# No dummy products at the attention's end, and one store for a tile's two left blocks

## The chip, the cores and the metric

The kernel runs on one core of one Trainium2 chip. The metric is the device time of one execution, in microseconds. TensorE (PE) multiplies matrices into PSUM, VectorE (DVE) and ScalarE (ACT) work on PSUM and SBUF, GpSimd (POOL) takes part in the attention, and SyncE (SP) and ScalarE issue DMAs from their queues.

## The reference

An attention with a feature map is followed by two MLPs, all in float32. It has 4 batches, 8 heads, 576 positions and 64 columns for each head; the MLPs see 2304 tokens of 512 features and have 2048 hidden features.

```python
def phi(x):
    proj = np.einsum('bhsd,df->bhsf', x, w_phi)
    proj = proj - np.max(np.abs(proj), axis=-1, keepdims=True)
    return np.concatenate([np.exp(proj), np.exp(-proj)], axis=-1)
q_p, k_p = (phi(q), phi(k))
kv = np.einsum('bhsf,bhsd->bhfd', k_p, v)
z = np.sum(k_p, axis=2)
num = np.einsum('bhsf,bhfd->bhsd', q_p, kv)
den = np.einsum('bhsf,bhf->bhs', q_p, z)[..., None] + 1e-06
x = num / den                                # then to (tokens, 512)
h = x @ w_in;  x = np.maximum(0.01 * h, h) @ w_out
h = x @ w2_in; y = (h * np.tanh(softplus(h))) @ w2_out
```

## The kernel before

**The attention** goes through 16 pairs of heads, `attention(n)` for n = 0 to 16, software-pipelined: a call does the projections of one pair, the sums of the next older and the output of the one before. A batch's first 512 positions are its main part; the last 64 are its left tokens. Products are made three times, from a high and a low part of each operand (`three`, L94 to L97), so that float32 is kept. `split`, `high` and `low` make the parts: a copy on ScalarE (L273) and a subtraction on VectorE (L277).

**The MLPs' products** are done by a seven-product scheme (Strassen-Winograd) over halves of features and tokens. An item n is one pair of 128-feature blocks f with one pair of batches sb. It uses four PSUM banks: X (product `p1`, A11 x B11), Z (`p7`, S3 x T3), Y and W. `seed_y` (ScalarE) copies X into Y; `keep_p7` (ScalarE) copies Z to SBUF (z7); `join_w` (VectorE) makes W = Y + z7. Then products are added on: S2 x T2 to Y and A12 x B21 to X (after which `head2` reads X out), A22 x T4 to W (`tail4`), S1 x T1 to Y (`tail5`, read out as Y + z7 by VectorE), S4 x B22 to Y (`tail3`). A read-out goes through the activation (`leaky`, L906) on ScalarE and is stored to DRAM by ScalarE's queue a step later. `c_item(f)` does the left tokens of all four batches, split into ch and cl, for the two blocks of f; it takes a bank of its own. The first items are (f, sb) = (0, 0), (1, 0), then c_item(0), c_item(1), then (0, 1), (1, 1).

**PSUM** has eight banks. During the attention, ring "a" has four, and the attention's own tiles the other four (pool `pa`); when the attention is done, these become ring "b" (pool `pb`). X, Z and the left tokens take ring "a", Y and W ring "b". A bank that is asked for when all of a ring are taken is one whose last reader must end first. The program order is the code's order on each engine; work that is not of the products (weight conversions, splits, sums, stores) is put between them in steps, by chains with costs and gates and by `later(n, f)`, which runs f n steps on.

**Around the attention's end.** In the last pairs' calls, `fill(0)` does p1 and p7 of item 0 and `fill(1)` its S2 x T2 and A12 x B21; `extra` (at == 1, n == PAIRS - 1) emits seed_y(0) and keep_p7(0). Behind the loop come p1(1), the last transposes `x_t(15)`, p7(1), and the release of the attention's pools. `touch(t)` is a dummy product of 512 columns into a bank, whose result is overwritten: one in fill(0) on item 0's Y, and four, L962 to L964, on the first four banks of ring "b". Then come seed_y(1), keep_p7(1), join_w(0), head2(0), and in `first` cycle(1): tail4(0), tail5(0), S2 x T2 and A12 x B21 of item 1, tail3(0), and c_item(0).

**The end.** The last products are those of the left tokens of the second MLP. A tile `left_out[t]` holds 128 rows: the 64 left tokens of batch 2t and those of batch 2t + 1. Its parts are added by VectorE (L1660), and `left_store(t)` stores it (L1666): rows 0 to 63 from SyncE's queue, rows 64 to 127 from ScalarE's. In DRAM the two blocks are 576 rows apart.

Of the kernel before, what the change touches and what calls it, by code (L numbers as in the profile page):

```python
# [9 lines left out]
F32 = mybir.dt.float32  # L10
F32R = mybir.dt.float32r
AF = mybir.ActivationFunctionType
ALU = mybir.AluOpType
# [7 lines left out]
def attention_two_mlps_kernel(  # L21
# [12 lines left out]
    nc = tc.nc  # L34
    B, H, S, D = q.shape
# [3 lines left out]
    P = 128  # L39
    KD = DM // P  # L40
    M = DFF // P
    MAIN = 512
    NM = MAIN // P
    LEFT = S - MAIN
# [26 lines left out]
    dr = tc.alloc_tile_pool(name="dr", bufs=1, space=bass.MemoryType.DRAM)  # L71
# [15 lines left out]
    def bank(ring):  # L87
        return rings[ring].tile([P, 512], F32, tag=ring, name=ring)
# [16 lines left out]
    class Places:  # L105
# [23 lines left out]
        def drop(self, t):  # L129
# [5 lines left out]
    places = Places([Places.Word(lambda i=i: two_words[:, i]) for i in range(2)] + [Places.Word(lambda: place("c", F32, DM, pool=gp))],  # L135
                    [Places.Word(lambda i=i: place("st%d" % i, I32, DM, 2, pool=gp, name="stage")) for i in range(2)])
# [111 lines left out]
    A11, A12, A22, S3, S1, S2, S4 = range(OPS)  # L248
# [32 lines left out]
    B11, T3, T2, B21, T1, T4, B22 = range(OPS)  # L281
    win = {}
# [27 lines left out]
    with tc.manual_schedule():  # L310
# [244 lines left out]
        def x_t(i):  # L555
            s = st[i]
            b, p = divmod(i, NP)
            t = pa.tile([P, 512], F32, tag="xt", name="xt")
            xn = s["xn"].rearrange("p c m d -> p (c m d)")
            for j in range(NM):  # L560
                nc.tensor.transpose(out=t[:, j * P:(j + 1) * P], identity=ident,  # L561
                                    in_=xn[:, j // 2 * 6 * D + j % 2 * P:][:, 0:P])
            o = st[min(i + 1, PAIRS - 1)]["kvp"][:, MAIN - LEFT:MAIN]
            nc.tensor.matmul(out=o, lhsT=xn[:, 4 * D:4 * D + P], rhs=eyes, start=True, stop=True)
            nc.scalar.activation(out=XC[:, p, b * LEFT:(b + 1) * LEFT], in_=o, func=AF.Copy)
            if i < PAIRS - 1:
                st[i] = None
            return lambda: nc.scalar.activation(out=xmain(p, b), in_=t, func=AF.Copy)
# [159 lines left out]
        def extra(n, at):  # L728
            for when, d in ((0, top), (1, mid), (2, end)):
                if at == when and n in d:  # L730
                    d[n]()
            for i, step in STEPS.get((n, at), ()):
                conv[i][step]()
            if at == 1 and n == PAIRS - 1:
                seed_y(0)
                keep_p7(0)

# [75 lines left out]
        def later(n, f):  # L815
            due.append((pos[0] + n, f))
# [9 lines left out]
        one = Layer()  # L826
# [4 lines left out]
        def weights(f, w):  # L831
            i, x = {A11: (0, 0), A12: (0, 1), A22: (1, 0), S3: (2, 0), S1: (2, 1), S2: (3, 0), S4: (3, 1)}[w]
            need(cur[0].mark[0], f, i)
            return [t[:, x * E:(x + 1) * E].rearrange("p (q n) -> p q n", q=2) for t in cur[0].wt[f, i]]
# [11 lines left out]
                three(t, h[:, i], l[:, i], xh[:, i], xl[:, i], start=(start and i == 0), stop=(i == 1),  # L846
                      skip_group_check=True)

        def touch(t):

            nc.tensor.matmul(out=t, lhsT=weights(0, A11)[0][:, 0], rhs=win[0, B11][0][:, 0],
                             start=True, stop=True)

        def p1(n):
            cur[0].it[n]["X"] = bank("a")
            prod(n, cur[0].it[n]["X"], A11, B11, True)

        def p7(n):
            cur[0].it[n]["Z"] = bank("a")
            prod(n, cur[0].it[n]["Z"], S3, T3, True)  # L860

        def seed_y(n):
            nc.scalar.activation(out=cur[0].it[n]["Y"], in_=cur[0].it[n]["X"], func=AF.Copy)

        def keep_p7(n):
            nc.scalar.activation(out=cur[0].z7[n % 2], in_=cur[0].it[n].pop("Z"), func=AF.Copy)

        def fill(part):
            if part == 0:
                p1(0)  # L870
                p7(0)
                it[0]["Y"] = bank("a")
                touch(it[0]["Y"])
            else:
                prod(0, it[0]["Y"], S2, T2, False)
                prod(0, it[0]["X"], A12, B21, False)
# [4 lines left out]
            attention(n)  # L881
        loads.held = False
        p1(1)
        x_t(PAIRS - 1)()
        p7(1)
        ap.release()
        pa.release()
        rings["b"] = tc.alloc_tile_pool(name="pb", bufs=4, space=PSUM)
# [31 lines left out]
        def join_w(n):  # L920
            x = cur[0].it[n]
            charge()
            nc.vector.tensor_tensor(out=x["W"], in0=x["Y"], in1=cur[0].z7[n % 2], op=ALU.add)
# [6 lines left out]
        def head2(n):  # L930
            cur[0].out((2 * cur[0].it[n]["f"], 2 * cur[0].it[n]["sb"]), cur[0].it[n]["X"])
# [13 lines left out]
        def c_half(f, t, i):  # L945
            need(cur[0].mark[1], "c", 0)
            need(cur[0].mark[1], "c", 1)
            b1, b2 = ([x[:, s] for x in cur[0].cw] for s in (slice(0, 2), slice(2, 4)))
            todo = [(w, o, q_) for w, o in (((A11, b1), (A12, b2)), ((S1, b1), (A22, cur[0].dw)))[i] for q_ in range(2)]
            for x, (w, o, q_) in enumerate(todo):  # L950
                h, l = weights(f, w)
                three(t[:, i * NC:(i + 1) * NC], h[:, q_], l[:, q_], o[0][:, q_], o[1][:, q_],
                      start=(x == 0), stop=(x == 3))

        def c_item(f, *between, g=None):
            t = bank("a")
# [2 lines left out]
                do()  # L959
            cur[0].out((f, B), t, g)  # L960

        it[0]["W"], it[1]["Y"], it[1]["W"], it[2]["Y"] = (bank("b") for _ in range(4))  # L962
        for t in (it[0]["W"], it[1]["Y"], it[1]["W"], it[2]["Y"]):
            touch(t)  # L964
        seed_y(1)
        keep_p7(1)
        join_w(0)
        head2(0)
        low(one.cw + [XC])
        nc.vector.tensor_tensor(out=XC[:, 0:2], in0=XC[:, 2:4], in1=XC[:, 0:2], op=ALU.subtract)  # L970

# [192 lines left out]
        def cycle(n):  # L1164
            it_ = cur[0].it
            x, begun = it_[n], "X" in it_[n]
            if n:
                tail4(n - 1)
                used(n - 1, 0, 1)
                work()  # L1170
            if not begun:
                p1(n)
            if "Y" not in x:
                x["Y"] = bank("b")
            if not begun:
                seed_y(n)
            work()
            if not begun:
                p7(n)
                keep_p7(n)  # L1180
            work()
            if n:
                tail5(n - 1)
                used(n - 1, 2)
                work()
            prod(n, x["Y"], S2, T2, False)
            if "W" not in x:
                x["W"] = bank("b")
            join_w(n)
            work()  # L1190
            prod(n, x["X"], A12, B21, False)
            head2(n)
            work()
            if n:
                tail3(n - 1)
                used(n - 1, 3)
                work()
# [462 lines left out]
            nc.vector.tensor_tensor(out=natural(left_out[t], h), in0=a, in1=b, op=ALU.add)  # L1660

        def left_store(t):
            o = left_out[t]
            for r in range(2):
                b = 2 * t + r
                (nc.sync, nc.scalar)[r].dma_start(out=out[b * S + MAIN:(b + 1) * S, :], in_=o[r * LEFT:(r + 1) * LEFT])  # L1666

        def left_shared():
            a, b = (work6("gh", "sums", F32).rearrange("p (a n) -> p a n", a=2) for _ in range(2))
# [154 lines left out]
```

## Time and profile before

| what | value |
|---|---|
| median of 3 runs | 883.2 us (883.2 to 883.5) |
| profiled execution | 883.12 us |
| its span, first to last instruction | 881.3 us |
| granted TensorE clock, mean | 0.999 |
| PE, DVE, ACT busy | 874.3, 633.3, 502.6 us |
| DMA | 197.28 MB, mean 224 GB/s |
| chain that ended last | PE 96%, ACT 2% |

A product of 512 columns shows as 0.39 us, but products are pipelined: the next begins before the end of the one before. So starts are compared, not durations. A start in a row is in us from the span's start. Behind the last instruction's work, the span ends when SyncE has seen all DMAs land and the engines have met at a barrier.

### The profile page before, as it was taken

Reading aid. Unit: us, or ns where it says so; the run is one execution under the profiler, and the core shown is the slowest. Engines: PE = TensorE matmul, PEld = TensorE weight load, DVE = VectorE, ACT = ScalarE, POOL = GpSimd, SP = SyncE. Lnnn points to the kernel's source line nnn. Section 1 sums busy time; section 2 is a strip of 40 time slices with the busy share of each in tenths; the row PEclk is TensorE's granted clock in tenths of the full one; section 3 lists DMA queues with packets and bytes.
Section 4 is the critical chain, followed back from the end, with each engine's and each line's share of the span. In section 5 each row is a group of like instructions: output and inputs, shape, how many; then the busy total and the mean of one; then the engine's idle time right before and its main releaser. Section 6 shows DMA issues by size and latency. Waiting matters only on the chain.

```text
span 881.3 us, 17024 instructions
## 1 busy us (share of the span) xinstructions
PE 874.3 (99%) x6497; PEld 754.1 (86%) x6497; DVE 633.3 (72%) x1056; ACT 502.6 (57%) x828; POOL 78.5 (9%) x62
## 2 busy tenths in 40 slices
PE   9999999999999999999999999999999999999997
PEld 7999999888888888888988888888888888888887
DVE  8999998688988626889886328676655488655575
ACT  6899998656565545544454326444444477444442
POOL 4646452000000000000000000000000000000000
PEclk9999999999999999999999999999999999999999
DMA  6653430179788867899962454888875899876662
GB/s 176 173 144 99 110 103 3 61 251 324 265 291 275 287 229 251 253 375 362 348 202 85 136 177 171 292 313 274 304 258 188 283 371 397 235 226 221 201 179 60
DMA packets 145585, 197.28 MB, mean 224 GB/s; under 512 B 50912, under 2 KB 82272, under 8 KB 145504
## 3 DMA queue, kind: packets, MB, share of 16 engines
q1 hardware_dynamic: 116096, 143.36, 50.6%
q10 hardware_dynamic: 29408, 52.84, 17.1%
q8 instruction: 51, 0.84, 0.4%
q14 instruction: 30, 0.25, 0.1%
HBM read 119.60 MB, written 76.55 MB: 223 GB/s over the span
## 4 chain that ended last, share of the span: by engine, by line
PE 96%; ACT 2%; DMA 0%; DVE 0%; issue 0%; SPq 0%; ACTq 0%
PE b L95 14%; PE b L97 14%; PE b L96 14%; PE a L95 13%; PE a L96 13%; PE a L97 13%; PE outs L535 3%; PE kvp L512 3%; PE a L469 1%; PE a L402 1%; PE a L441 1%; PE xt L441 1%; PE xt L561 1%; PE kvp L515 1%; ACT qp L454 0%; ACT kp L454 0%
## 5 line engine op out<-in xcount | busy, mean ns | idle before, releaser
L92 DVE TENSOR_TENSOR g<-raw,g 128x1024 fp32r<-128x1024 f32 (+1 forms) x64 | 77.1, 1205 | 54.4 <-ACT g L91 54.3
L91 ACT ACTIVATE g<-raw 128x1024 fp32r<-128x1024 f32 (+1 forms) x64 | 66.9, 1046 | 66.5 <-PE b L97 37.0
L92 DVE TENSOR_TENSOR gl<-raw,gh 128x512 fp32r<-128x512 f32 x72 | 49.7, 690 | 60.0 <-ACT gh L91 57.7
L91 ACT ACTIVATE gh<-raw 128x512 fp32r<-128x512 f32 x72 | 45.2, 628 | 60.8 <-PE b L97 24.6
L473 POOL PARTITION_ALL_REDUCE qm<-qd x30 | 64.2, 2189 | 45.1 <-ACT qd L471 42.1
L96 PE MATMUL b<-gl,wo 128*128 128x512 f32 (+1 forms) x192 | 67.9, 354 | 0.0
L95 PE MATMUL b<-gh,wo 128*128 128x512 f32 (+1 forms) x192 | 67.9, 354 | 0.0
L97 PE MATMUL b<-gh,wo 128*128 128x512 f32 (+1 forms) x192 | 67.9, 354 | 0.0
L95 PE MATMUL b<-win,w 128*128 128x512 f32 x128 | 49.9, 390 | 0.0
L96 PE MATMUL b<-win,w 128*128 128x512 f32 x128 | 49.9, 390 | 0.0
L95 PE MATMUL a<-gh,wo 128*128 128x512 f32 x128 | 49.8, 389 | 0.0
L96 PE MATMUL a<-gl,wo 128*128 128x512 f32 x128 | 49.8, 389 | 0.0
L97 PE MATMUL a<-gh,wo 128*128 128x512 f32 x128 | 49.8, 389 | 0.0
L97 PE MATMUL b<-win,w 128*128 128x512 f32 x128 | 49.8, 389 | 0.0
L95 PE MATMUL b<-g,wo 128*128 128x512 f32 x128 | 49.8, 389 | 0.0
L96 PE MATMUL b<-g,wo 128*128 128x512 f32 x128 | 49.8, 389 | 0.0
L97 PE MATMUL b<-g,wo 128*128 128x512 f32 x128 | 49.8, 389 | 0.0
L917 DVE TENSOR_TENSOR g<-b,z 128x512 f32<-128x512 f32 x31 | 21.4, 689 | 36.2 <-PE b L97 33.4
L96 PEld LDWEIGHTS b<-gl,wo 128*128 128x128 f32 x192 | 36.3, 189 | 5.0
L97 PEld LDWEIGHTS b<-gh,wo 128*128 128x128 f32 x192 | 36.3, 189 | 5.0
L95 PEld LDWEIGHTS b<-gh,wo 128*128 128x128 f32 x192 | 36.3, 189 | 4.9
L1514 DVE TENSOR_TENSOR g<-g,g 128x512 f32<-128x512 f32 x32 | 22.1, 689 | 23.0 <-ACT g L1498 16.5
(325 smaller groups left out, 2535.5 us busy)
## 6 DMA issues: line engine op xcount, KB each, us to landing
raw<-gp SPq DMA_DIRECT2D x56, 512.0 KB, 5.4
raw<-gd ACTq DMA_DIRECT2D x72, 256.0 KB, 3.8
gd<-g ACTq DMA_DIRECT2D x70, 256.0 KB, 3.9
stage<-in_moe_w_out_dram SPq DMA_DIRECT2D x32, 512.0 KB, 5.6
gp<-g SPq DMA_DIRECT2D x64, 256.0 KB, 2.8
stage<-in_moe_w_in_dram SPq DMA_DIRECT2D x26, 512.0 KB, 6.0
gp<-g ACTq DMA_DIRECT2D x48, 256.0 KB, 3.1
scr<-more SPq DMA_DIRECT2D x24, 256.0 KB, 5.1
```

The lines of the kernel that those rows point to most:

```text
L91: nc.scalar.activation(out=hi, in_=src, func=AF.Copy)
L92: nc.vector.tensor_tensor(out=lo, in0=src, in1=hi.bitcast(F32), op=ALU.subtract)
L95: nc.tensor.matmul(out=o, lhsT=wh_, rhs=xh, start=start, stop=False, **kw)
L96: nc.tensor.matmul(out=o, lhsT=wh_, rhs=xl, start=False, stop=False, **kw)
L97: nc.tensor.matmul(out=o, lhsT=wl_, rhs=xh, start=False, stop=stop, **kw)
L402: nc.tensor.transpose(out=t[:, j * P:(j + 1) * P], in_=s[nm + "n"].rearrange("p h t d -> p (h t d)")[:, j * P:(j + 1) * P], identity=ident)
L441: nc.tensor.matmul(out=t[:, j * 2 * F:(j + 1) * 2 * F], lhsT=s[x][:, u], rhs=w, start=(n == 0 and j == 0), stop=(n == 2), skip_group_check ...
L473: nc.gpsimd.partition_all_reduce(qm, qd, P, bass_isa.ReduceOp.absmax)
L512: nc.tensor.matmul(out=both[r, h, a, :], lhsT=s["kp"][a][:, h, t, r], rhs=s["vm"][:, h, t, :], start=(a == 0 and h == 0 and t == 0), stop= ...
L535: nc.tensor.matmul(out=g[u // 2][r, u % 2, h], lhsT=s["qp"][a][:, h, q0 + r.start:q0 + r.stop], rhs=s["kv"][:, 2 * h + a], start=(a == 0), ...
L917: nc.vector.tensor_tensor(out=c, in0=x["Y"], in1=cur[0].z7[n % 2], op=ALU.add)
L1514: nc.vector.tensor_tensor(out=out_, in0=in0, in1=in1, op=ALU.subtract)
```

## The change

Three things. First, `touch` and its five uses are gone. Item 0's Y and W, and item 1's Y and W, come from ring "a" during the attention's end; item 0's Y takes the bank that keep_p7(0) has emptied, so seed_y(0) stands behind keep_p7(0). The same holds for item 1: join_w(0), keep_p7(1) and seed_y(1) are emitted before the attention's pools are released. item 0's X is read out by one ScalarE pass into `first_out`, a tile of the weight-staging places, right behind p1(1), and stored from there. Items 2 and 3 have the rings swapped (X and Z in "b"), and all later ones are as before (`ring`). Second, in `c_half` the second half's first product doesn't carry the start flag. Third, `left_store(t)` is one DMA on SyncE's queue, from 128 rows to 2 x 64.

```diff
@@ -732,8 +732,10 @@
             for i, step in STEPS.get((n, at), ()):
                 conv[i][step]()
             if at == 1 and n == PAIRS - 1:
+                it[1]["X"], it[1]["Z"] = (bank("a") for _ in range(2))
+                keep_p7(0)
+                it[0]["Y"] = bank("a")
                 seed_y(0)
-                keep_p7(0)
 
 
 
@@ -846,17 +848,18 @@
                 three(t, h[:, i], l[:, i], xh[:, i], xl[:, i], start=(start and i == 0), stop=(i == 1),
                       skip_group_check=True)
 
-        def touch(t):
-
-            nc.tensor.matmul(out=t, lhsT=weights(0, A11)[0][:, 0], rhs=win[0, B11][0][:, 0],
-                             start=True, stop=True)
+        def ring(n, of):
+
+            return bank("ab"[(of in "YW") != (cur[0] is one and n < 4 and (n > 1 or of in "YW"))])
 
         def p1(n):
-            cur[0].it[n]["X"] = bank("a")
+            if "X" not in cur[0].it[n]:
+                cur[0].it[n]["X"] = ring(n, "X")
             prod(n, cur[0].it[n]["X"], A11, B11, True)
 
         def p7(n):
-            cur[0].it[n]["Z"] = bank("a")
+            if "Z" not in cur[0].it[n]:
+                cur[0].it[n]["Z"] = ring(n, "Z")
             prod(n, cur[0].it[n]["Z"], S3, T3, True)
 
         def seed_y(n):
@@ -869,8 +872,6 @@
             if part == 0:
                 p1(0)
                 p7(0)
-                it[0]["Y"] = bank("a")
-                touch(it[0]["Y"])
             else:
                 prod(0, it[0]["Y"], S2, T2, False)
                 prod(0, it[0]["X"], A12, B21, False)
@@ -881,8 +882,15 @@
             attention(n)
         loads.held = False
         p1(1)
+        first_out = places.take(places.words)
+        nc.scalar.activation(out=first_out, in_=it[0]["X"], func=AF.Prelu, alpha=0.01)
         x_t(PAIRS - 1)()
         p7(1)
+        it[0]["W"] = bank("a")
+        nc.vector.tensor_tensor(out=it[0]["W"], in0=it[0]["Y"], in1=one.z7[0], op=ALU.add)
+        keep_p7(1)
+        it[1]["Y"] = bank("a")
+        seed_y(1)
         ap.release()
         pa.release()
         rings["b"] = tc.alloc_tile_pool(name="pb", bufs=4, space=PSUM)
@@ -950,7 +958,7 @@
             for x, (w, o, q_) in enumerate(todo):
                 h, l = weights(f, w)
                 three(t[:, i * NC:(i + 1) * NC], h[:, q_], l[:, q_], o[0][:, q_], o[1][:, q_],
-                      start=(x == 0), stop=(x == 3))
+                      start=(x == 0 and i == 0), stop=(x == 3), skip_group_check=True)
 
         def c_item(f, *between, g=None):
             t = bank("a")
@@ -959,13 +967,9 @@
                 do()
             cur[0].out((f, B), t, g)
 
-        it[0]["W"], it[1]["Y"], it[1]["W"], it[2]["Y"] = (bank("b") for _ in range(4))
-        for t in (it[0]["W"], it[1]["Y"], it[1]["W"], it[2]["Y"]):
-            touch(t)
-        seed_y(1)
-        keep_p7(1)
-        join_w(0)
-        head2(0)
+        gd[0, 0] = dr.tile([P, MAIN], F32, name="gd0_0")
+        later(1, lambda: nc.scalar.dma_start(out=gd[0, 0], in_=first_out))
+        later(8, lambda: places.drop(first_out))
         low(one.cw + [XC])
         nc.vector.tensor_tensor(out=XC[:, 0:2], in0=XC[:, 2:4], in1=XC[:, 0:2], op=ALU.subtract)
 
@@ -1171,7 +1175,7 @@
             if not begun:
                 p1(n)
             if "Y" not in x:
-                x["Y"] = bank("b")
+                x["Y"] = ring(n, "Y")
             if not begun:
                 seed_y(n)
             work()
@@ -1185,7 +1189,7 @@
                 work()
             prod(n, x["Y"], S2, T2, False)
             if "W" not in x:
-                x["W"] = bank("b")
+                x["W"] = ring(n, "W")
             join_w(n)
             work()
             prod(n, x["X"], A12, B21, False)
@@ -1660,10 +1664,8 @@
             nc.vector.tensor_tensor(out=natural(left_out[t], h), in0=a, in1=b, op=ALU.add)
 
         def left_store(t):
-            o = left_out[t]
-            for r in range(2):
-                b = 2 * t + r
-                (nc.sync, nc.scalar)[r].dma_start(out=out[b * S + MAIN:(b + 1) * S, :], in_=o[r * LEFT:(r + 1) * LEFT])
+            dst = out[2 * t * S:2 * (t + 1) * S].rearrange("(r s) n -> r s n", s=S)[:, MAIN:S]
+            nc.sync.dma_start(out=dst, in_=left_out[t])
 
         def left_shared():
             a, b = (work6("gh", "sums", F32).rearrange("p (a n) -> p a n", a=2) for _ in range(2))
```

TensorE, from p7(1) to tail4(0) (whose operands are v_3032 and v_3033 before, v_3030 and v_3031 now, into W), before:

```order
L95 MATMUL a<-v_2585,x_1_3151 128x512
L96 MATMUL a<-v_2586,x_1_3151 128x512
L97 MATMUL a<-v_2585,x_1_3151 128x512
L851 MATMUL b<-v_1452,a_1065 128x512 x4
L95 MATMUL b<-v_3032,a_1067 128x512
L96 MATMUL b<-v_3033,a_1067 128x512
L97 MATMUL b<-v_3032,a_1067 128x512
```

and now:

```order
L95 MATMUL a<-v_2585,x_1_3152 128x512
L96 MATMUL a<-v_2586,x_1_3152 128x512
L97 MATMUL a<-v_2585,x_1_3152 128x512
L95 MATMUL a<-v_3030,a_1067 128x512
L96 MATMUL a<-v_3031,a_1067 128x512
L97 MATMUL a<-v_3030,a_1067 128x512
```

The four dummies are gone, and W lies in ring "a".

ScalarE, from the copy of the last transposes (xc, x) to the split of the second pair of batches (s), before; L863 is seed_y, L866 keep_p7:

```order
L565 ACTIVATE xc<-kvp 128x64
L568 ACTIVATE x_1_3149<-xt 128x512
L273 ACTIVATE ch<-xc 128x1024
L863 ACTIVATE b<-a 128x512
L866 ACTIVATE z_76<-a 128x512
L906 ACTIVATE g<-a 128x512
L906 ACTIVATE g<-b 128x512
L908 DMA gd_0_3244<-g 128x512
L908 DMA gd_0_3255<-g 128x512
L273 ACTIVATE s_3258<-x_0_2203 128x1024
```

and now; L886 is the pass into first_out, L869 keep_p7, L866 seed_y, L914 the activation:

```order
L886 ACTIVATE c<-a 128x512
L565 ACTIVATE xc<-kvp 128x64
L568 ACTIVATE x_1_3150<-xt 128x512
L869 ACTIVATE z_76<-a 128x512
L866 ACTIVATE a<-a 128x512
L273 ACTIVATE ch<-xc 128x1024
L914 ACTIVATE g<-a 128x512
L971 DMA gd_0_3236<-c 128x512
L916 DMA gd_0_3247<-g 128x512
L273 ACTIVATE s_3250<-x_0_2203 128x1024
```

The read-out of item 0's X has moved ahead of the last transposes, and ch has moved behind keep_p7 and seed_y, which have changed places.

SyncE, the program's end, before (ScalarE's queue ends with one such row, `L1666 DMA out_dram<-o 64x512 x2`, for its two stores):

```order
L1540 DMA raw_9754<-gl_8241 128x512
L1540 DMA raw_9785<-gl_8466 128x512
L1608 DMA out_dram<-o_9713 128x4x64 x4
L1666 DMA out_dram<-o 64x512 x2
L1819 UNCONDITIONAL_BRANCH
```

and now, with nothing of it on ScalarE's queue:

```order
L1544 DMA raw_9748<-gl_8235 128x512
L1544 DMA raw_9779<-gl_8460 128x512
L1612 DMA out_dram<-o_9707 128x4x64 x4
L1668 DMA out_dram<-o 2x64x512 x2
L1821 UNCONDITIONAL_BRANCH
```

Two stores of 64 rows on each of two queues have become two of 2 x 64 rows on one.

## Rows read from the trace of the kernel before

**Rows 1.** The page, section 1: busy us, share of the span, instructions of each engine.
```profile
PE 874.3 (99%) x6497; PEld 754.1 (86%) x6497; DVE 633.3 (72%) x1056; ACT 502.6 (57%) x828; POOL 78.5 (9%) x62
```

**Rows 2.** Busy us (instructions) of PE, PEld, DVE, ACT, POOL in one stretch; clock; DMA.
```profile
172.00:870.00 698.00, 697.96 (x3397) 591.26 (x3396) 477.54 (x776) 354.98 (x559) 0.00 (x0) 1.00 0.76 255
```

**Rows 3.** The first dummy product: ns min/median/max, first and last start us.
```profile
L851 PE MATMUL a<-v,a x1: 392/392/392, 147.2 to 147.2; 128*128 128x512 f32 x1
```

**Rows 4.** Timeline, TensorE: start us, us, engine, line, tile, shape, count.
```profile
162.09 0.39 PE L97 MATMUL a<-v,x 128*128 128x512 f32 x1
...
162.32 1.07 PE L851 MATMUL b<-v,a 128*128 128x512 f32 x4
...
163.50 0.50 PE L95 MATMUL b<-v,a 128*128 128x512 f32 x1
...
163.84 0.39 PE L96 MATMUL b<-v,a 128*128 128x512 f32 x1
...
164.76 0.39 PE L97 MATMUL b<-v,a 128*128 128x512 f32 x1
...
169.17 0.50 PE L95 MATMUL a<-v,a 128*128 128x512 f32 x1
...
170.66 0.28 PE L95 MATMUL a<-ch,a 128*128 128x256 f32 x1
```

**Rows 5.** Timeline, ScalarE and its queue; in brackets idle before and releaser.
```profile
163.02 0.58 ACT L863 ACTIVATE b<-a 128x512 f32<-128x512 f32 x1 [0.28 <-ACT ch L273]
...
163.51 0.59 ACT L866 ACTIVATE z<-a 128x512 f32<-128x512 f32 x1
...
165.19 0.60 ACT L906 ACTIVATE g<-b 128x512 f32<-128x512 f32 x1 [0.60 <-PE b L97]
...
165.20 0.95 ACTq L908 DMA_DIRECT2D gd<-g  x2
...
166.19 2.01 ACT L273 ACTIVATE s<-x 128x1024 fp32r<-128x1024 f32 x2 [0.40 <-ACT g L906]
...
170.64 0.57 ACT L906 ACTIVATE g<-a 128x512 f32<-128x512 f32 x1
```

**Rows 6.** Timeline, VectorE, the same stretch.
```profile
162.75 0.70 DVE L923 TENSOR_TENSOR b<-a,z 128x512 f32<-128x512 f32 x1 [2.65 <-PE b L851]
...
167.29 1.23 DVE L277 TENSOR_TENSOR s<-x,s 128x1024 fp32r<-128x1024 f32 x1 [1.99 <-ACT s L273]
...
168.43 0.68 DVE L917 TENSOR_TENSOR g<-a,z 128x512 f32<-128x512 f32 x1
```

**Rows 7.** Timeline, VectorE, the last addition; then SyncE's queue, the left blocks' stores.
```profile
876.94 0.42 DVE L1660 TENSOR_TENSOR o<-sums,b 128x256 f32<-128x256 f32 x1 [0.29 <-PE b L97]
...
876.67 1.22 SPq L1666 DMA_DIRECT2D out_dram<-o  x2
```

**Rows 8.** Left store line, last pair, SyncE's half: issue ns, landing us after issue.
```profile
L1666 SPq DMA_DIRECT2D out_dram<-o x1: 500/500/500, 877.4 to 877.4; - x1
...
DMA to landing us min/median/max: 2.3/2.3/2.3
```

**Rows 9.** The same pair, ScalarE's half.
```profile
L1666 ACTq DMA_DIRECT2D out_dram<-o x1: 712/712/712, 877.4 to 877.4; - x1
...
DMA to landing us min/median/max: 2.9/2.9/2.9
```

**Rows 10.** DMA, 877.4 to 880.4, in 40 slices: busy tenths, GB/s, packets; queues.
```profile
DMA  0000045897949849999999973779794330000000
GB/s 0 0 0 0 0 109 137 218 273 137 300 82 218 164 109 356 437 437 437 410 410 382 355 246 110 246 218 300 246 273 137 109 137 0 0 0 0 0 0 0
DMA packets 320, 0.52 MB, mean 175 GB/s; under 512 B 64, under 2 KB 64, under 8 KB 320
...
q1 hardware_dynamic: 160, 0.26, 33.4%
...
q10 hardware_dynamic: 160, 0.26, 26.5%
```

## The prediction

> **What bounds the kernel now.** I read the page's busy times first. TensorE is busy for 874.3 of 881.3 us [rows 1], and in the long stretch from 172 to 870 us it is busy for 697.96 of 698.00 us at a granted clock of 1.00, the upper level of 2.4 GHz [rows 2]. So nothing that the other engines do matters in that stretch as long as each product's inputs and its bank are there in time. The end of the run moves with the start of this stretch, at about 170.66 us, and with what comes behind the last product. The change touches just these two places. I read the timelines of the three compute engines at the first [rows 3 to 6], and the last addition, the stores behind it and the DMA slices at the second [rows 7 to 10]. The profiled execution took 883.12 us for a span of 881.3; the median of the runs is 883.2, so I add changes to the one and get the other within 0.1 us.
>
> **The dummy products.** Four of them stand at 162.32 us, and their 1.07 us are three steps and the last one's 0.39, so a step is (1.07 - 0.39) / 3 = 0.227 us [rows 4]. A fifth stands in the last head pair's round, at 147.2 [rows 3]. Five steps are 1.13 us of TensorE. Behind the four, TensorE's first real product waits until 163.50: VectorE's addition that seeds its bank starts only when a dummy has ended, at 162.75, after 2.65 us of idleness, and takes 0.70 [rows 4, 6]. From the last dummy's end of its step, 162.32 + 4 x 0.227 = 163.23, that wait is 0.27. After a wait, the first product holds the next back by 0.34 instead of 0.23 us (163.50 to 163.84) [rows 4], so each wait costs 0.11 more. Without dummies the addition can run right behind VectorE's last normalisation, about 160 us, and has 2 us to spare. tail4(0) then starts one step behind p7(1)'s last product, at 162.09 - 0.23 + 0.23 = 162.09 instead of 163.50. That is 1.41 us earlier, and 1.52 with the restart. This would be the gain if nothing else came due.
>
> **What comes due next is ScalarE.** Its order changes. Now it must first copy Z away (keep_p7), then seed Y into the bank that Z leaves, and only then come to the split of the left tokens (ch). Step by step: p7(1)'s last product starts at 161.86, and ScalarE reads a product's bank 0.43 after its last start (164.76 to 165.19) [rows 4, 5], so at 162.29. The copy takes 0.59, and the seed writes the same bank and waits for its end: 162.9. One 128x512 pass later, 0.49 (163.02 to 163.51) [rows 5], ch starts at 163.4. The 128x1024 pass holds ScalarE about twice as long, 0.95, so tail4(0)'s output follows at 164.35. Behind it stand two store issues, as before, and the split s starts 1.00 after that output (165.19 to 166.19) [rows 5]: 165.35 instead of 166.19. ScalarE gains 0.84 us, not 1.52. VectorE's split waits for s (1.99 us of idleness before 167.29), and the addition at 168.43 stands behind it in VectorE's queue [rows 6]; tail3(0), at 169.17 [rows 4], waits for that addition, since it overwrites its input. It comes 0.84 earlier, at 168.33.
>
> **A new wait.** The four banks of the one ring now hold X1, Y0, Y1 and W1 when c_item(0) asks for one, where before W and Y had banks of the other ring. It must wait until head2(1) has read X1. That pass runs from 170.64 to 171.21 now [rows 5], and 0.84 earlier in the change: it ends at 170.37. c_item(0) starts at 170.41, as against 170.66 [rows 4]. TensorE would be ready at 168.33 + 0.11 + 6 x 0.23 = 169.82, so it waits 0.6. Queued behind it is the whole rest of TensorE's stream. After the restart (0.11) the stream is 0.25 - 0.11 = 0.14 us earlier than before. I take -0.14 for this part. Its bounds are +0.1, if the seed or ch takes 0.2 longer than I read, and -1.5, if the wait does not bind.
>
> **The rest of the first part** costs nothing that I can find: first_out is one pass of 0.6 us between 158 and 161 us, where ScalarE has nothing to do before the last transposes; its store keeps its place among the issues; the swapped rings of the third and fourth item keep every later bank's reader at least 0.5 us ahead of TensorE in the times of before, more than the 0.14 by which TensorE moves.
>
> **The store at the end.** The last addition ends at 877.36 [rows 7]. Two stores of 64 rows are issued there on two queues. SyncE's lands 2.3 us after its issue [rows 8], ScalarE's 2.9 [rows 9], at 880.3, and 1.0 later the span ends. The change issues one store of 2 x 64 rows on SyncE instead, and has another of the same kind 0.72 before it, in place of the first pair. What does such a store cost? A row of 2 KB takes one DMA engine between 75 and 99 ns: in the fullest slices 16 engines move 437 GB/s, 27.3 each, which is 75 ns, and ScalarE's queue needed 26.5% of 16 engines in 3.0 us = 12.7 us for its 128 rows, 99 ns with 32 closing packets in it [rows 10]. I take 85. The open question is over how many engines the rows go. In rows 10 the four stores have 64 packets under 512 B among 320, that is sixteen closings for each store of 64 rows: sixteen engines, each with four of the leading 64. Every transfer of the kernel before leads, in its code, with a count that sixteen divides (32, 64, 128 or 512) on both sides. The new one leads with 2 on its DRAM side and has the 64 behind it; no row shows such a transfer. If the rows are dealt out in equal shares of the leading count, there are two shares, one for each block, and two engines. If the second count is dealt out too, there are sixteen.
>
> With sixteen: 128 x 85 / 16 = 0.7 us, already in the 2.3 to 2.9 of rows 8 and 9. With two: 64 x 85 ns = 5.4 us for a store, and both stores queue on the same two engines, as their shape and queue are the same: 10.9 us. The first slice with DMA work is the sixth, at 877.8, in a pair issued at 876.67 [rows 7, 10]; the change comes 0.14 earlier. So 877.65 + 10.9 = 888.55 for the last row, 0.4 to the landing (the last busy slice ends at 879.9, and the last store lands at 880.3), 1.0 to the end and one more step of SyncE's closing waits, some 0.06: 890.0. That is +8.7 to the span. With 75 and 99 ns a row it is +7.4 and +10.5.
>
> The sixteen engines are the lower end and the two the upper. I take the upper: sharing by the leading count explains the sixteen closings of rows 10 with nothing added, while the other reading needs the chip to look at a second count, of which no row shows a trace. The Trainium skill, "DMA: Bandwidth & Descriptors", section "Why a DMA increments its semaphore by 16 and not by 1", says that the number of engines is the largest one up to 16 which divides the outermost size of both sides, and that these are the lowest-numbered ones: two here, the same two for both stores, and so the 10.9 us. In the trace only the sixteens agree with it; no run here shows a smaller number.
>
> **Sum.** -0.14 at the attention's end is already in the 877.65; +8.7 in all: 883.12 + 8.7 = 891.8 us.
>
> **The rivals.** First, the store goes over sixteen engines. Then SyncE alone lands like its half of before, 2.3 to 2.9 us after the issue at 877.25: 879.55 to 880.15 instead of 880.3. The gain there is 0.15 to 0.75, less the 0.06; I take 0.4. With the 0.14 it is 883.12 - 0.54 = 882.6, not slower. The slower half on ScalarE's queue speaks for this gain [rows 8, 9]. The skill's same page, section "Rules for kernel authors", speaks for the merging too: it advises one 128-partition transfer in place of two to disjoint halves. By that rule alone the result would be this 882.6. Second, two engines for each store, but not the same two: the second store's rows begin at 877.25 + 1.1 and take 5.4, so 883.8, and with 0.4 and 1.06 the span ends at 885.3: 883.12 + 4.0 = 887.1. Third, sixteen engines, and the wait for X1's bank does not bind: 883.12 - 1.5 - 0.4 = 881.2. Against it stands that c_item(0) finds all four banks held.
>
> **How the numbers follow.** Two engines, the same for both: 0.75. Two engines each: 0.07. Sixteen with the small gain: 0.16. Sixteen with the full gain: 0.02. The measurement of this kernel can tell about 0.2%, 1.8 us, from no change: faster is below 881.4, slower above 885.0. So slower has 0.75 + 0.07 = 0.82, same 0.16, faster 0.02. The range from 886.5 to 893.7 holds the first two cases with the bounds of the row's time (the second case with 75 ns is 886.5), and leaves out 0.18.
>
> **What would show it.** In the profile after, the stores of 2 x 64 rows should have two closings each, not sixteen; the DMA slices behind 877 should show about 2/16 of the engines busy, one tenth, for 11 us at some 48 GB/s; the last landing should come about 11 us after the last addition. At 162 us the addition should start near 160 and tail4(0) near 162.1; TensorE should wait near 168 for VectorE and until about 170.4 for ScalarE's read of X1. A landing within 3 us of its issue, with sixteen closings, would make the prediction wrong; so would c_item(0) starting before 169.9 for the first part alone.

## The result, and the profile after

The changed kernel takes 892.5 us (median of 5 runs, 892.4 to 892.6) as against 883.2 us: 1.0106 times as long, with a 95% interval of 1.0094 to 1.0117. The forecast was 891.8, in a range from 886.5 to 893.7, with two engines for the store as the cause. The profiled execution took 892.38 us for a span of 890.6.

The page's busy times, and the long stretch, answer [rows 1] and [rows 2]:

```profile
PE 873.3 (98%) x6492; PEld 753.1 (85%) x6492; DVE 632.8 (71%) x1056; ACT 502.4 (56%) x828; POOL 78.5 (9%) x62
```
```profile
172.00:870.00 698.00, 697.96 (x3397) 591.25 (x3396) 476.36 (x776) 354.48 (x558) 0.00 (x0) 1.00 0.76 255
```

TensorE has five products less and is 1.0 us less busy. In the long stretch it is as full as before. So nothing was lost in there, and the 9.3 us by which the span grew must lie at its ends.

**The attention's end.** Two executions don't begin alike. A step far ahead of the change shows by how much: in the chain that ended last, the same head pair's outputs begin at 139.86 us before and at 139.63 after.

```profile
139.86 2.02 PE outs L535 x64
```
```profile
139.63 2.02 PE outs L535 x64
```

So 0.23 us has to be added to the times of after, to set them beside [rows 4 to 6]. TensorE's timeline after (L535 is the last head pair's outputs; in brackets idle time and what ended it):

```profile
155.79 2.08 PE L535 MATMUL outs<-kv,qp 128*64 128x65 f32 x64
...
161.65 0.39 PE L97 MATMUL a<-v,x 128*128 128x512 f32 x1
161.87 0.39 PE L95 MATMUL a<-v,a 128*128 128x512 f32 x1
...
168.11 0.50 PE L95 MATMUL a<-v,a 128*128 128x512 f32 x1 [0.61 <-DVE g L925]
...
170.21 0.39 PE L95 MATMUL a<-ch,a 128*128 128x256 f32 x1 [0.43 <-ACT g L914]
170.43 0.28 PE L96 MATMUL a<-cl,a 128*128 128x256 f32 x1
```

tail4(0) follows p7(1) by one step, at 161.87, so the wait behind the dummies is gone. Then come two waits: tail3(0) for VectorE, and c_item(0) for ScalarE's L914, which is head2(1), the read of X1. ScalarE and VectorE in the same stretch:

```profile
162.07 0.60 ACT L869 ACTIVATE z<-a 128x512 f32<-128x512 f32 x1 [0.74 <-PE a L97]
162.70 0.58 ACT L866 ACTIVATE a<-a 128x512 f32<-128x512 f32 x1
163.19 1.05 ACT L273 ACTIVATE ch<-xc 128x1024 fp32r<-128x1024 f32 x1
...
164.14 0.59 ACT L914 ACTIVATE g<-a 128x512 f32<-128x512 f32 x1
...
165.13 2.01 ACT L273 ACTIVATE s<-x 128x1024 fp32r<-128x1024 f32 x2 [0.40 <-ACT g L914]
...
169.58 0.57 ACT L914 ACTIVATE g<-a 128x512 f32<-128x512 f32 x1
```
```profile
159.56 0.69 DVE L890 TENSOR_TENSOR a<-a,z 128x512 f32<-128x512 f32 x1
...
166.23 1.23 DVE L277 TENSOR_TENSOR s<-x,s 128x1024 fp32r<-128x1024 f32 x1
167.37 0.68 DVE L925 TENSOR_TENSOR g<-a,z 128x512 f32<-128x512 f32 x1
```

From the last pair's outputs to c_item(0) it is 14.42 us (155.79 to 170.21). In the kernel before it was 14.42 as well (156.24 in the row below, to 170.66 in [rows 4]):

```profile
156.24 2.08 PE L535 MATMUL outs<-kv,qp 128*64 128x65 f32 x64
```

The four dummies' 0.9 us and the wait behind them went into the two new waits. What c_item(0) has still gained against the step at 139.86 is 0.22 us. That is the one step of the fifth dummy, which lay ahead of those outputs.

**The end.** The stores' issues on SyncE's queue and VectorE's last addition, in the timeline; then the DMA slices from 876 to 892 us (40 slices of 0.4 us: busy share of 16 engines in tenths, GB/s, packets, queue q1):

```profile
876.32 1.28 SPq L1668 DMA_DIRECT2D out_dram<-o  x2
876.59 0.42 DVE L1664 TENSOR_TENSOR o<-sums,b 128x256 f32<-128x256 f32 x1 [0.29 <-PE b L97]
```
```profile
DMA  0000111101111111111111111111111100000000
GB/s 0 0 0 10 20 20 41 31 31 10 46 46 51 51 51 51 51 51 51 51 51 51 51 51 51 51 51 51 51 51 51 51 31 0 0 0 0 0 0 0
DMA packets 260, 0.52 MB, mean 33 GB/s; under 512 B 4, under 2 KB 4, under 8 KB 260
...
q1 hardware_dynamic: 260, 0.52, 9.4%
```

The last addition ends at 877.01. After that no compute engine has work, and still the span lasts 13.6 us more; in [rows 7] it was 4.0. In all but one slice one tenth of the engines is busy, from 877.5 to 889.1, at 10 to 46 GB/s until 880.8 and at 51 behind that. Where [rows 10] have 64 packets under 512 B, the closings of sixteen engines for four stores (a closing is the small packet with which an engine ends its share), there are 4 now: two engines for each of two stores. The queue's 9.4% of 16 engines in 16 us are 24.1 us, or 94 ns for each of the 256 rows.

### The profile page after: what moved, and what is told of

The parts are those of the page before. It is cut to its first block, busy times and chain, and to the rows that moved or that the text cites. A ratio compares the mean times of both kernels' runs of the same rounds, so it can differ in the third digit from the quotient of the medians.

```text
span 890.6 us, 17012 instructions
## 1 busy us (share of the span) xinstructions
PE 873.3 (98%) x6492; PEld 753.1 (85%) x6492; DVE 632.8 (71%) x1056; ACT 502.4 (56%) x828; POOL 78.5 (9%) x62
## 4 chain that ended last, share of the span: by engine, by line
PE 95%; ACT 3%; DVE 0%; issue 0%; ACTq 0%
PE b L95 14%; PE b L96 14%; PE b L97 14%; PE a L95 13%; PE a L96 13%; PE a L97 13%; PE outs L535 3%; PE kvp L512 3%; PE a L402 1%; PE a L469 1%; PE a L441 1%; PE xt L441 1%; PE xt L561 1%; PE kvp L515 1%; ACT qp L454 0%; ACT kp L454 0%
## 5 line engine op out<-in xcount | busy, mean ns | idle before, releaser
L925 DVE TENSOR_TENSOR g<-b,z 128x512 f32<-128x512 f32 x28 | 19.3, 689 | 36.5 <-PE b L97 35.3
```

The costliest lines, as they stand in the source:

```text
L925: nc.vector.tensor_tensor(out=c, in0=x["Y"], in1=cur[0].z7[n % 2], op=ALU.add)
```

## The experiments

Times in the texts below are medians. What was expected is quoted as it was put on record ahead of each run.

### One part alone

**The new attention's end alone** (the changed kernel with the stores of before; the dummies' removal, the new banks and the start flag are all in it):

```diff
         def left_store(t):
-            dst = out[2 * t * S:2 * (t + 1) * S].rearrange("(r s) n -> r s n", s=S)[:, MAIN:S]
-            nc.sync.dma_start(out=dst, in_=left_out[t])
+            o = left_out[t]
+            for r in range(2):
+                b = 2 * t + r
+                (nc.sync, nc.scalar)[r].dma_start(out=out[b * S + MAIN:(b + 1) * S, :], in_=o[r * LEFT:(r + 1) * LEFT])
```

> The changed attention's end alone; the left blocks are stored as before, 64 rows from each of two queues. Theory (the prediction): the start of the steady stretch moves by -0.14 us against a run that began alike, so 883.0 us, which is no change that can be measured; c_item(0) starts near 170.2 to 170.4, having waited for ScalarE's read of X1, and the end is as before, some 4.0 us behind the last addition. Rival 1: the new wait is not there in other runs and the full 1.5 us are gained, 881.7. Rival 2: part of the 9.3 us lost comes from the attention's end, then it is 884 or more.

Measured: 883.2 us, ratio 1.000 (0.9991 to 1.0008), no change that can be told. TensorE's timeline shows the same two waits, and c_item(0) 14.41 us behind the last pair's outputs:

```profile
156.07 2.08 PE L535 MATMUL outs<-kv,qp 128*64 128x65 f32 x64
...
168.39 0.50 PE L95 MATMUL a<-v,a 128*128 128x512 f32 x1 [0.64 <-DVE g L925]
...
170.48 0.38 PE L95 MATMUL a<-ch,a 128*128 128x256 f32 x1 [0.44 <-ACT g L914]
```

What the change does beside the store costs nothing, which takes away rival 2. The full gain of rival 1 isn't there either.

**The store alone** (the kernel before with only the new `left_store`, the same lines the other way round):

> The kernel before with nothing but the one store for two left blocks. Theory: the whole loss is in the store, +9.2 to 9.5 us, 892.5 us, with two closing packets for each store and 5.1 to 6.5 us of rows for each. Rival: the loss needs the new attention's end too (other buffers, other queue state), then it is below 891.

Measured: 892.8 us, ratio 1.0114 (1.0098 to 1.0129). Its last microseconds read as those of the changed kernel:

```profile
DMA  0000011110111111111111111111111110000000
...
DMA packets 260, 0.52 MB, mean 33 GB/s; under 512 B 4, under 2 KB 4, under 8 KB 260
```

The whole loss is in the store.

### Is it the leading count?

The new store differs from the old in more than its leading count of 2: it has three dimensions, it jumps by 1.18 MB, and all 256 rows go by one queue. The next two runs keep two dimensions, contiguous pieces and both queues, and change only how many stores there are and how many rows each has. Each block of 64 is cut in two (in the second run 60 stands for 62):

```diff
             for r in range(2):
                 b = 2 * t + r
-                (nc.sync, nc.scalar)[r].dma_start(out=out[b * S + MAIN:(b + 1) * S, :], in_=o[r * LEFT:(r + 1) * LEFT])
+                for i, j in ((0, 62), (62, LEFT)):
+                    (nc.sync, nc.scalar)[r].dma_start(out=out[b * S + MAIN + i:b * S + MAIN + j, :],
+                                                      in_=o[r * LEFT + i:r * LEFT + j])
```

> The changed attention's end; each block of 64 left rows goes, on the queue it had before, as a store of 62 rows and one of 2. Each destination is one contiguous piece with two dimensions, and both queues are used. Theory (equal shares of the leading count over a number of engines up to sixteen that divides it): 62 = 2 x 31, so two engines, 31 rows each, and the 2 rows on two engines: 32 rows for a block, four blocks. If the same two engines serve both queues that is 128 rows x 90 ns = 11.5 us, 892 to 893 us in all; if each queue has other engines, 64 rows, 5.8 us, 886.5 to 887.5. Rival 1 (the loss is from the two blocks lying 1.18 MB apart, or from the third dimension): nothing is lost but two more issues on each queue, 883.0 to 884.0. Rival 2 (the loss is from one queue carrying 256 rows): the same 883.0 to 884.0.

> As the run with 62 and 2 rows, but 60 and 4. Theory: 60 = 15 x 4, so fifteen engines with four rows each, then four engines with one: the rows take about 0.5 us, and the time is 883.0 to 884.0, with 15 and 4 closing packets. Rival (any store whose leading count is not a multiple of sixteen is dealt to few engines, or that more and smaller stores cost by themselves): as slow as the run with 62 rows.

Measured: 893.2 us with 62 and 2 (ratio 1.0115, 1.0101 to 1.0128), and 883.05 with 60 and 4 (0.9998, 0.9989 to 1.0007). The DMA slices from 876 to 892 us, first with 62 and 2:

```profile
DMA  0000000011011111111111111111111111110000
...
DMA packets 272, 0.52 MB, mean 33 GB/s; under 512 B 16, under 2 KB 16, under 8 KB 272
...
q10 hardware_dynamic: 136, 0.26, 4.9%
q1 hardware_dynamic: 136, 0.26, 4.7%
```

and with 60 and 4:

```profile
DMA  0006888820000000000000000000000000000000
...
DMA packets 332, 0.52 MB, mean 33 GB/s; under 512 B 76, under 2 KB 76, under 8 KB 332
```

The closings count the engines. With 62 and 2 there are 16 for eight stores: two each. With 60 and 4 there are 76, which is 4 x (15 + 4). So the count of engines is the largest divisor of the leading count up to sixteen, in all cases tried here: 2, 4, 15 and 16. With 62 rows in the long store instead of 60, the same bytes take 10 us more. The rivals of both runs fall. The run with 62 rows shows one thing more: its two queues (q1 SyncE, q10 ScalarE) together take some 12 us, no less than the one queue of the changed kernel, and are one tenth busy. On different engines they would be two tenths busy for half the time, so both queues put their shares on the same two engines. The Trainium skill, "DMA: Bandwidth & Descriptors", section "Why a DMA increments its semaphore by 16 and not by 1", has this rule, lowest-numbered engines and all; these runs agree with its counts, though which engines they are no row tells.

**One such store instead of two** (the first tile as before, the last one by one store of 2 x 64):

```diff
-            dst = out[2 * t * S:2 * (t + 1) * S].rearrange("(r s) n -> r s n", s=S)[:, MAIN:S]
-            nc.sync.dma_start(out=dst, in_=left_out[t])
+            if t == 1:
+                dst = out[2 * t * S:2 * (t + 1) * S].rearrange("(r s) n -> r s n", s=S)[:, MAIN:S]
+                nc.sync.dma_start(out=dst, in_=left_out[t])
+            else:
+                o = left_out[t]
+                for r in range(2):
+                    b = 2 * t + r
+                    (nc.sync, nc.scalar)[r].dma_start(out=out[b * S + MAIN:(b + 1) * S, :], in_=o[r * LEFT:(r + 1) * LEFT])
```

> The changed attention's end; the first tile is stored as before (64 rows from each of two queues), only the last one by one store of 2 x 64 rows. Theory: half of the 256 rows go to the two engines, 64 rows each at 90 ns = 5.8 us, which begin some 1.2 us behind the issue at 877.1: 884.1, and 1.5 to the end of the span, 885.6, so 887.4 us: the second half of the loss was the second store standing behind the first on the same two engines. Rival: a store of 2 x 64 rows costs about 9 us by itself (a fixed price of its form, not rows in a queue), then about 892.

Measured: 888.5 us, ratio 1.0058 (1.004 to 1.0077). There are 34 closings: 16, 16 and 2. The DMA slices, as above:

```profile
GB/s 0 0 0 0 20 200 236 215 26 20 20 26 51 51 51 51 51 51 51 51 51 51 36 0 0 0 0 0 0 0 0 0 0 0 0 0 0 0 0 0
DMA packets 290, 0.52 MB, mean 33 GB/s; under 512 B 34, under 2 KB 34, under 8 KB 290
```

The rival's 892 is out: the price is by rows in a queue, not by form. But 887.4 was 1.1 us too low. The GB/s show where: for 1.6 us the rate is 20 to 26, half of what follows. The first rows of such a store are slower. It is so in the changed kernel too, whose rate is 10 to 46 until 880.8 and 51 from there. Why, no run here tells.

**One store and sixteen engines.** The tile's rows alternate between the two batches, so that DRAM leads with 64 and has the 2 behind it. The split of the left tokens' parts reads them in that order:

```diff
-            dst = out[2 * t * S:2 * (t + 1) * S].rearrange("(r s) n -> r s n", s=S)[:, MAIN:S]
+            dst = out[2 * t * S:2 * (t + 1) * S].rearrange("(r s) n -> s r n", s=S)[MAIN:S]
             nc.sync.dma_start(out=dst, in_=left_out[t])
...
-                    split(*hl, raw)
+                    if steps3[s][0] == 2:
+                        split(*(x.rearrange("p (n s r) -> p n s r", n=OPS, r=2) for x in hl),
+                              raw.rearrange("p (n r s) -> p n s r", n=OPS, r=2))
+                    else:
+                        split(*hl, raw)
```

> The changed attention's end and one store for a tile on SyncE's queue, but the tile's 128 rows alternate between the two batches (the split of the left tokens' parts reads them in that order), so that the DRAM side leads with 64 and has the 2 behind it. Same bytes, same rows, same queue, same number of stores. Theory (the leading count decides): sixteen engines, sixteen closing packets for a store, landing 2.3 to 2.9 us after the issue: 882.5 to 883.2 us. Rival (the second count, the jump of 1.18 MB between rows, or 256 rows on one queue is what costs): 888 to 893 us.

Measured: 882.8 us, ratio 0.9997 (0.9988 to 1.0006).

```profile
878.39 0.42 DVE L1668 TENSOR_TENSOR o<-sums,b 128x256 f32<-128x256 f32 x1 [0.29 <-PE b L97]
```
```profile
DMA  0000000049990000000000000000000000000000
...
DMA packets 288, 0.52 MB, mean 33 GB/s; under 512 B 32, under 2 KB 32, under 8 KB 288
...
out_dram<-o SPq DMA_DIRECT2D x2, 256.0 KB, 2.5
```

It has the same bytes, queue and number of stores as the changed kernel, more jumps of 1.18 MB (at every row), and 32 closings instead of 4; the 9 us are gone. From the last addition's end to the end of the span it is 3.6 us (878.81 to 882.4) instead of 4.0: the small gain of the first rival. By itself it is too small to be told in the times.

### Where the dummies' gain went

The dummies' end was to give up to 1.5 us and gave none that can be measured. The theory names two waits that took its place. Each can be taken away by order alone. First, ScalarE's read of X1 is emitted ahead of a split that stood before it (in `cycle`, for n == 1 of the first MLP alone, as it then reads; `work()` emits splits):

```diff
             if n:
                 tail5(n - 1)
                 used(n - 1, 2)
-                work()
             prod(n, x["Y"], S2, T2, False)
...
             join_w(n)
-            work()
             prod(n, x["X"], A12, B21, False)
             head2(n)
             work()
+            work()
+            work()
```

> The changed attention's end with the stores of before, and head2(1), ScalarE's read of X1, emitted ahead of one split that stood before it. Theory (c_item(0) waits for X1's bank): X1's last product is there at 167.54, ScalarE is free at 167.66, the read ends at 168.25, and c_item(0) starts right behind tail3(0), near 169.6 instead of 170.2 to 170.5 in the same run's time: -0.6 to -0.7 us against the change without it, 882.5 us. tail3(0) still waits 0.6 us for VectorE. Rival (something else holds c_item(0), as cl or the weights): no change, 883.2.

Measured: 883.0 us (0.9998, 0.9989 to 1.0007). In the trace c_item(0) comes 13.82 us behind the last pair's outputs instead of 14.41, with no wait of its own; tail3(0)'s wait has stayed.

```profile
155.91 2.08 PE L535 MATMUL outs<-kv,qp 128*64 128x65 f32 x64
...
168.24 0.50 PE L95 MATMUL a<-v,a 128*128 128x512 f32 x1 [0.62 <-DVE g L925]
...
169.73 0.28 PE L95 MATMUL a<-ch,a 128*128 128x256 f32 x1
```

The mechanism is as the theory says. The time alone doesn't show it, since 0.6 us is less than can be told: it is nearer to the rival's 883.2 than to the 882.5 that was expected. Second, with the first kept, tail5(0)'s products and addition also go ahead of the `work()` that emits the split s (again for n == 1 alone; the 4 is how many `work()` later the sum's activation comes, so that it doesn't hold ScalarE):

```diff
                 tail4(n - 1)
                 used(n - 1, 0, 1)
+                tail5(n - 1, 4)
+                used(n - 1, 2)
                 work()
...
-            if n:
-                tail5(n - 1)
-                used(n - 1, 2)
```

> As the run with X1 read early, and tail5(0)'s addition on VectorE stands ahead of the split s that held it. Theory (these two waits are all that stands between the removed dummies and their full gain): the addition runs from 166.2 to 166.9, tail3(0) starts one step behind A12 x B21 at 167.3, c_item(0) at 168.7; TensorE doesn't wait from 160.4 on. -1.5 us against the change without both, 881.7 us. Rival (the next thing comes due: W1, dl or a split is late by as much): 882.5 or more.

Measured: 882.35 us, ratio 0.9988 (0.998 to 0.9997), which lies between the theory's 881.7 and the rival's 882.5. c_item(0) is 12.90 us behind the last pair's outputs, 1.5 earlier than without both, as expected. But part of it was given back some 15 us later. TensorE:

```profile
156.05 2.09 PE L535 MATMUL outs<-kv,qp 128*64 128x65 f32 x64
...
168.95 0.28 PE L95 MATMUL a<-ch,a 128*128 128x256 f32 x1
```
```profile
185.04 0.50 PE L95 MATMUL a<-s,a 128*128 128x512 f32 x1 [0.36 <-DVE a L931]
```

ScalarE and its queue ahead of it (L866 is seed_y of the third item):

```profile
176.70 2.82 ACTq L916 DMA_DIRECT2D gd<-g  x2
...
179.57 0.58 ACT L866 ACTIVATE a<-b 128x512 f32<-128x512 f32 x1 [2.41 <-PE b L97]
```

Two issues of stores held ScalarE's queue for 2.82 us, one of them for 2.33; in the changed kernel the same two took 1.05, with a gap between them:

```profile
177.65 1.05 ACTq L916 DMA_DIRECT2D gd<-g  x2
```

seed_y stood behind them, VectorE's join_w (L931) came late in turn, and at 185.04 TensorE waited for it. Up to there some 0.9 us were given back. This execution, at 883.64 us one of the slower ones of its kernel, lost about 1.2 us more in waits at 328.02 and 718.43. Other kernels' traces wait near those places too (at 329.80 with 62 rows, at 719.41 with the alternating rows), so these two don't belong to the edit. To see whether the long issue was chance, the same kernel ran once more, and also together with the alternating rows:

> The run with the two waits taken away, once more, with the stores of before, for a second trace: if the issue of 2.33 us is chance, the steady stretch is ahead by the whole 1.5 us, and the span of this profile is near 880; if it belongs to the order, the same 0.9 us are given back at 180 to 185 us.

> The two waits taken away (X1 read early, the addition ahead of the split) together with one store for a tile whose rows alternate between the batches. If the two add up: 882.35 of the run with the waits away, less 0.4 for the landing (3.57 us from the last addition's end to the span's end instead of 3.97): 881.9 us, faster than the kernel before by 0.15%. In the trace c_item(0) starts 12.9 us behind the last head pair's outputs, as against 14.4 before. If the one issue on ScalarE's queue that took 2.33 us in the run with the waits away (at 176.7, where it takes 0.33 in the others) belongs to the new order, it is there again, and some 0.9 us are given back by 185 us; if it was chance, it is gone and the stretch to the last product is 1.5 us ahead.

Measured: 881.4 us for the same kernel again (0.9985, 0.9976 to 0.9994), and 881.4 us with the alternating rows (0.9981, 0.9972 to 0.9989). Both intervals end below 1; the last median is the lowest here, 1.7 us below the kernel before. But the two medians of the same kernel, 882.35 and 881.41, lie 0.9 us apart, so a difference of that size shows little by itself. The two issues again, in the second trace of the same kernel and then in that with alternating rows:

```profile
176.13 2.24 ACTq L916 DMA_DIRECT2D gd<-g  x2
```
```profile
176.36 0.87 ACTq L916 DMA_DIRECT2D gd<-g  x2
```

and TensorE, first in the second trace of the same kernel, then with the alternating rows:

```profile
183.46 0.39 PE L97 MATMUL a<-v,x 128*128 128x512 f32 x1
183.88 0.50 PE L95 MATMUL a<-s,a 128*128 128x512 f32 x1
```
```profile
155.71 2.09 PE L535 MATMUL outs<-kv,qp 128*64 128x65 f32 x64
...
168.61 0.28 PE L95 MATMUL a<-ch,a 128*128 128x256 f32 x1
```

They take 2.82, 2.24 and 0.87 us in three executions whose order on ScalarE is the same there. So a long issue isn't fixed by that order; it came in two of the three, and what makes it long is open. In the one with 2.24 the product at 183.88 comes 0.42 behind the one before it instead of 0.23, so less is given back than in the first. In the one with 0.87 nothing is given back: c_item(0) is 12.90 us behind the outputs, and TensorE has no wait between there and 707 us. That the two gains add up isn't shown by the medians (881.41 and 881.36); the trace shows each in its place.

## Why the prediction was right, point by point

**The bound.** Right. The stretch from 172 to 870 us is unchanged, and the time moved with its start and with what lies behind the last product.

**The dummies and ScalarE's order.** Right, step by step. With the 0.23 us by which this execution was ahead, keep_p7(1) was forecast at 162.29 and came at 162.30, ch at 163.4 and 163.42, tail4(0)'s output at 164.35 and 164.37, s at 165.35 and 165.36, tail3(0) at 168.33 and 168.34.

**The new wait.** Right: c_item(0) was forecast at 170.41 and came at 170.44, held by the read of X1. At the last addition the stream is 0.35 us ahead (876.59 as against 876.94), of which 0.23 is the execution's and 0.12 the change's; 0.14 was forecast. The runs that took the waits away showed that both were real. The 1.5 us that then appeared between the last pair's outputs and c_item(0) are as many as the sum had before "what comes due", but that is in part luck. The sum's 1.52 has the fifth dummy's 0.23 in it, which lies ahead of those outputs, so 1.29 is left of it there. The rest is a wait for VectorE that tail3(0) already had in the kernel before and that the sum left out (at 169.17 in [rows 4], 0.32 us from the product before it instead of 0.23, and 0.11 behind it):

```profile
168.85 0.39 PE L97 MATMUL a<-v,x 128*128 128x512 f32 x1
```

The bound of -1.5 "if the wait does not bind" was wrong by itself: with X1's wait alone taken away, c_item(0) came only 0.6 us earlier.

**The engines of the store.** Right, and the choice that mattered. Nothing in the trace of before showed fewer than sixteen. The forecast rested on sixteen closings for a leading count of 64, and the runs with 62, 60 and alternating rows have now shown the rule for other counts.

**The size of the store.** A little small. 128 rows in a row on an engine were put at 85 ns each, 10.9 us; they took 11.6 (877.5 to 889.1), 90 ns each. The slower first rows are the difference, and more: from 880.8 on, 51 GB/s on two engines are 80 ns a row. The term was taken from stores in which sixteen engines share the work. Its bounds of 75 and 99 ns also left one queue out: SyncE's, the one that the change uses, shows 33.4% in [rows 10], which by the same sum is 125 ns, so the range was drawn too narrow at its upper end. The result fell inside it all the same. The 1.46 us behind the last row held: 889.1 to 890.6. So the span grew by 9.3 us instead of 8.7, and the time is 892.5 instead of 891.8.

**The rivals.** Sixteen engines came only when the DRAM side led with 64, and then gave the 882.8 that the first rival had put at 882.6. Two different engines for the two stores are out, since the second store's rows follow the first's. The full gain of the third needed the two waits gone.

## What to carry to other kernels

Before two DMAs are merged into one, look at the outermost count of both sides as they are written: a merged 2 x 64 is dealt to two engines, 64 x 2 to sixteen. Where dummy work is removed from a bound engine, follow the other engines' queues to the next thing that engine needs: here the gain was there only once ScalarE's read and VectorE's addition had been moved ahead of splits that could wait. And a store at the program's end has no work to hide behind, so its rows per engine are paid in full.

## What the runs showed of the hardware that was not expected

- SyncE's and ScalarE's queues share the few engines of a narrow store: with 62 and 2 rows, two queues are no faster than one (24.6 us of engine time, 9.6% of sixteen engines in 16 us, on two engines; 24.1 us with one queue).
- The first rows of a two-engine store move at 10 to 46 GB/s, the later ones at 51; a store of 64 rows for an engine added some 5.1 us alone as the last one, and some 4.5 more when another stood ahead of it (4.0, 9.1 and 13.6 us from the last addition to the end of the span).
- A DMA issue on ScalarE's queue that takes 0.33 us in most traces took 2.33 us once and 1.47 once, and held the pass behind it.
